# An mLSTM and feed-forward kernel on one core: the opening's 414 steps in another order, with more of the low parts and of the state's decay on GpSimd

## The chip, the core and the metric

The kernel runs on one core of a Trainium2 chip. It has five engines that each run their own instructions in order and wait for each other by semaphores: TensorE (PE, with its weight loads as PEld), VectorE (DVE), ScalarE (ACT), GpSimd (POOL) and SyncE (SP), which here issues nearly all transfers. The metric is the time of one execution in microseconds, the median of several runs; lower is better.

## The reference

First an mLSTM over 4 batches, 8 heads, 768 steps and head size 40, with a stabilised exponential gate; then a feed-forward layer over its 3072 tokens of 320 values.

```python
for t in range(S):
    m_new = np.maximum(f_gate[:, :, t] + m, i_gate[:, :, t])
    f_stab = np.exp(f_gate[:, :, t] + m - m_new)
    i_stab = np.exp(i_gate[:, :, t] - m_new)
    m = m_new
    C = f_stab[:, :, None, None] * C + i_stab[:, :, None, None] * np.einsum('bhd,bhe->bhde', vt, kt)
    n = f_stab[:, :, None] * n + i_stab[:, :, None] * kt
    h_tilde = np.einsum('bhde,bhe->bhd', C, qt)
    denom = np.maximum(np.abs(np.einsum('bhd,bhd->bh', n, qt)[:, :, None]), 1.0)
    y[:, :, t] = 1.0 / (1.0 + np.exp(-o_gate[:, :, t])) * h_tilde / denom
...
x = y.transpose(0, 2, 1, 3).reshape(B * S, H * D)
h = x @ w_in                                            # 3072 x 2048
g = np.maximum(h, 0.0) + alpha * np.minimum(h, 0.0)
out = (g @ w_out).astype(np.float32)                    # 3072 x 320
```

`w_in`, `w_out` and `alpha` take part in double precision in the reference; the weights arrive in DRAM as 8-byte numbers.

## The kernel before

**Tiling.** The recurrence is done by chunks of 128 steps: 6 chunks a batch, 24 in all. Within a chunk the scores (keys times queries, by head) are multiplied by a matrix of decays E and applied to the values; what came earlier enters through the state C. Two chunks make a group of 256 tokens; there are 12 groups, and each goes through the feed-forward layer in 8 pairs of 256 hidden values: an up projection (16 matmuls into a tile `ph`), the activation into `g`, and a down projection (12 matmuls into `po`).

**Precision by parts.** Operands of the feed-forward layer are split into a high part and the rest, the low part (`XH`, `XL`; `WH`, `WL`, and `W2` for the last 64 rows of `w_in`; `OH`, `OL`; `gh`, `gl`), and three products of parts are summed. A low part is one subtraction (`low`, line 891, for weights; line 785 for the products' `gl`). Weights come as two 32-bit words: ScalarE scales the high word (`scale`, line 855), then either scales the low word too (`three`, line 865), or VectorE shifts the high one (`shift`, line 871), and VectorE joins both (`join`, lines 877 and 879).

**Order.** Nothing is left to a scheduler. `ORDER` is a string of names; each name stands for a step that issues some instructions, and every engine runs its instructions in the order in which the steps issue them. After `ORDER`, which covers the first batch (chunks 0 to 5) and the first group or two of the feed-forward layer, a repeating `PATTERN` supplies the rest of the order for chunks 6 to 23 and the other groups; a step that `ORDER` has named isn't repeated. The names that matter here, with n the chunk and p the pair of hidden blocks:

- `dq`n, `dv`n, `dL`, `do` load queries and keys, values, decays and output gates. `i`, `r` and `o` with their numbers are blocks of `w_in`, of its last 64 rows, and of `w_out`: `d` loads a block, `s` scales, `x` or `y` is the choice above, `j` joins, `h` and `H` write a high part, `l` and `L` a low part on VectorE, `p` and `P` a low part on GpSimd.
- `qT`n, `kT`n transpose queries and keys on TensorE, `qc`n, `kc`n copy them out on ScalarE. `sp` spreads the decays over the partitions on TensorE (chunks 0 to 3), `ex` takes their exponential, `sc` makes scores, `wg` multiplies them by E, `v`n applies them to the values, `fm`n and `ft`n take the state's part, `ta`n adds both.
- `wd`n weighs the keys, `um`n and `uc`n update the state with them; `uc`n first multiplies the old state by its decay, on the engine that the set `CP` names.
- `gr`, `gg`, `gx`, `gp` gate chunk n: the reciprocal, the gate, the product (`XNP` names the chunks whose product is GpSimd's), and a copy on GpSimd. `x`n transposes the chunk's x on TensorE; `xa`n writes `XH`, `xd`n writes `XL`.
- `U` or `V` with group and pair is an up projection; `R S G K` or `r s g N` follow: the negative part on ScalarE, the activation on VectorE, the high part on ScalarE, and the low part, on VectorE for `K` and on GpSimd for `N`. `D` is the down projection.

**PSUM.** Most small matmul results of the opening take their tile from `psa`, from two tags of two buffers each; a buffer is free again once its last reader is done. Untagged requests alternate between the tags.

Of the kernel before, what the change touches and what calls it, by code (L numbers as in the profile page):

```python
# [17 lines left out]
def kernel(ctx: ExitStack, tc: tile.TileContext, q, k, v, i_gate, f_gate, o_gate, w_in, w_out, alpha, out):  # L18
# [397 lines left out]
    def gated_steps(n, hv):  # L416
# [21 lines left out]
        if b == 0:  # L438
            nc.vector.scalar_tensor_tensor(out=sg, in0=sg, scalar=1.0, in1=rb, op0=ALU.add, op1=ALU.mult)
        else:  # L440
            nc.gpsimd.tensor_tensor(sg, sg, rb, ALU.mult)
# [214 lines left out]
    def first_stacks():  # L656
# [28 lines left out]
    ORDER = """warm18 kfz alT lf0z warm2 warm2 i00d i00s sca0 lf0a lf0b dq0 L0 sp01 qT0 dq1 alC li0 bj0 wt0 bTt kT0 i00x qc0 kc0 ewj
        i01d sca1 bTc ex01 sp00 sc00 qT1 wTt eeL wTc qc1 wd0 li1 lf1a lf1b kT1 sc01 i00j ex00 kc1 eTt Cz eTc sp11 ex11
        dv0 wg01 i01s wd1 L1 um0 uc0 i01x lpa um1 sp10 wg00 gma gmd ex10 i01j i00h fm1 ft1 sc11 do0 sc10 wg10 bj1 wtl
        blt ewl blc i00p o0d o0s r0d o0x gmm gmc r0s r0x v0 wg11 lpb lpc lpd uc1 dq2 qT2 o2d gr0 wlt og1 warm2 wlc r0j
        i11d lpe o0j i01h i01p gg0 qc2 dq3 gx0 gp0 kT2 v1 eel elt elc sp21 kc2 sc21 dL r0H ta1 gr1 gg1 sp20 ex21 qT3
        wg21 i10d dv1 r0h gx1 gp1 r0p r0L ex20 wd2 sc20 wg20 qc3 x0 x1 xa0 xd0 dq4 fm2 wd3 xa1 xd1 i10s F0 ft2 o2s o2y  # L690
        sp31 o0h ex31 kT3 o2j o2h i10y i10j um2 U00 o0l V01 kc3 R00 i11s uc2 i11y i11j o2l do1 i10h i10l sp30 r01 qT4
        qc4 ex30 S00 v2 sc31 i20d i20s ta2 gr2 i20x wg31 o1d og2 gg2 gx2 kT4 i20j kc4 sc30 wg30 G00 K00 i21d fm3 ft3
        s01 i20h o1s i20p i11h i11p o1x r2d o1j i21s i21x sc41 v3 um3 i21j uc3 ta3 dL4 U02 V03 r2s r2y o3d gr3 sc40
        ex41 fm4 R02 dq5 o1h o1l o4d g01 r2j N01 qT5 i21h i21p o3s S02 o3x G02 K02 dL5 wg41 i31d ft4 D00 wd4 dq6 o3j
        qc5 dv2 r2h r2p r03 ex40 o4s r2H D01 o4x gg3 s03 o3h o4j gx3 o5d gp3 wg40 i30d V04 r04 s04 dv3 o4h V05 gp2 x2
        x3 xa2 xd2 o6d do2 wd6 kT5 g04 r2P g03 o3l xa3 r05 o4l s05 v4 xd3 kc5 i31s ta4 N03 N04 i31y i31j i30s o5s o5x
        F1 V10 gr4 r10 um4 uc4 dL6 i30x um6 U11 ex50 R11 o5j s10 uc6 S11 ex51 g10 i31h dL7 i31p sc50 N10 i30j dq7 wg50
        U12 fm5 ft5 o5h sc51 wg51 v5 o7d R12 S12 ta5 D10 G11 K11 o6s o6x gr5 og3 gg5 G12 gx5 gg4 D11 K12 D12 i30h i30l
        gx4 U13 gp5 D02 tp0 do3 U06 o7s gp4 o5l o6j vp0 R13 tp1 g05 S13 G13 N05 K13 o7x o6h D13 vp1 o7j U07 tp2 tp3
        R06 S06 R07 x4 x5 xa5 xd5 D03 D04 D05 S07 o7h o7l G06 K06 o6l D06 xa4 xd4 G07 K07 D07 Z0"""  # L700
# [36 lines left out]
    class FeedForward:  # L737

        def __init__(self, g):
            self.g, self.x, self.done, self.named = g, x_tiles.pop(g), [], 0  # L740
# [4 lines left out]
        def up(self):  # L745
            for step in self.up_steps(self.g < 2):
                pass

        def up_steps(self, split=True):
            g, fp = self.g, self.named  # L750
            self.named += 1
# [34 lines left out]
            self.done.append((gh, gl))  # L786
# [580 lines left out]
```

## Time and profile before

| | |
|---|---|
| median of 3 runs | 465.4 us (465.05 to 465.82) |
| the profiled execution | 465.35 us, its span 463.6 us |
| granted TensorE clock | 0.998 |
| busy: PE, DVE, ACT, POOL | 452.8, 329.8, 315.0, 308.4 us |
| transfers | 68.67 MB, mean 148 GB/s |

Busy time is that of the span from the first to the last instruction on the core; the execution's own time has 1.75 us more around it. A busy TensorE is not one at its peak, since the ends of matmuls are modelled and overlap. The opening, up to the step that ends `ORDER`, covers about the first 105 us.

### The profile page before, as it was taken

The numbers are of one execution on the slowest core, as the hardware profiler recorded it, in microseconds if no ns is written. First come the engines' busy times: TensorE is split into PE (matmuls) and PEld (weight loads), VectorE is DVE, ScalarE is ACT, GpSimd is POOL, SyncE is SP. The second block draws the span as 40 slices with busy tenths as digits, with TensorE's granted clock in tenths as the row PEclk, the third lists the DMA queues.
The fourth block names the chain that finished last, engine by engine and source line by source line (L and its number), as shares of the span: only waits on it lengthen the run. The fifth ranks groups of instructions, "written<-read, shape, count | busy, mean of one in ns | idle before, by whom it ended". The sixth has DMA issues, their size and how long they took to land.

```text
span 463.6 us, 11813 instructions
## 1 busy us (share of the span) xinstructions
PE 452.8 (98%) x4366; PEld 442.0 (95%) x4366; DVE 329.8 (71%) x692; ACT 315.0 (68%) x707; POOL 308.4 (67%) x377
## 2 busy tenths in 40 slices
PE   8989989999999999999999999999999999999996
PEld 6879978999999999999999999999999999999996
DVE  4989998747776787886875887886776786764321
ACT  4899898676857858758856958757857858423331
POOL 8551674854698697588888598588888686324231
PEclk9999999999999999999999999999999999999999
DMA  9999994869775775888997686688796463020000
GB/s 184 177 221 252 277 252 118 175 122 190 151 182 147 138 184 160 137 174 173 158 187 176 122 197 168 133 166 180 153 206 156 107 154 90 1 84 15 28 2 28
DMA packets 186306, 68.67 MB, mean 148 GB/s; under 512 B 150234, under 2 KB 178506, under 8 KB 186250
## 3 DMA queue, kind: packets, MB, share of 16 engines
q1 hardware_dynamic: 186170, 67.83, 67.2%
q8 instruction: 34, 0.56, 0.5%
q14 instruction: 22, 0.18, 0.2%
q10 hardware_dynamic: 80, 0.11, 0.1%
HBM read 40.44 MB, written 7.57 MB: 104 GB/s over the span
## 4 chain that ended last, share of the span: by engine, by line
PE 83%; DVE 5%; DMA 5%; SPq 3%; ACT 3%; issue 1%; ACTq 0%; DVEq 0%
PE po L796 36%; PE ph L759 5%; PE ph L765 5%; PE ph L762 5%; PE ph L760 5%; PE ph L761 5%; PE ph L764 4%; PE ph L763 4%; PE ph L766 4%; PE pH L377 4%; PE pS L515 4%; DMA wi<-in_moe_w_in_dram 2%; DMA wr<-in_moe_w_in_dram 2%; PE pI L403 1%; PE pu L203 1%; DMA qn<-in_q_dram 1%
## 5 line engine op out<-in xcount | busy, mean ns | idle before, releaser
L785 POOL TENSOR_TENSOR gl<-g,gh 128x512 fp32r<-128x512 f32 x77 | 100.5, 1306 | 42.9 <-ACT gh L783 39.6
L796 PE MATMUL po<-OH,gh 128*128 128x320 f32 x368 | 110.7, 312 | 0.0
L796 PE MATMUL po<-OL,gh 128*128 128x320 f32 x368 | 109.3, 309 | 0.0
L769 ACT ACTIVATE g<-ph 128x512 f32<-128x512 f32 x96 | 57.1, 596 | 58.2 <-PE ph L766 56.0
L774 DVE SCALAR_TENSOR_TENSOR g<-g,oma,ph 128x256 f32<-128x256 f32 x156 | 66.8, 469 | 32.7 <-ACT g L769 32.3
L796 PEld LDWEIGHTS po<-OL,gh 128*128 128x128 f32 x368 | 69.2, 188 | 0.1
L796 PEld LDWEIGHTS po<-OH,gh 128*128 128x128 f32 x368 | 69.1, 188 | 0.0
L796 PE MATMUL po<-OH,gl 128*128 128x320 f32 x368 | 69.0, 309 | 0.0
L759 PE MATMUL ph<-XH,WH 128*128 128x256 f32 x192 | 57.2, 298 | 1.1 <-ACT wo L865 0.7
L796 PEld LDWEIGHTS po<-OH,gl 128*128 128x128 f32 x368 | 57.9, 188 | 0.0
L764 PE MATMUL ph<-XL,WH 128*128 128x256 f32 x192 | 54.3, 283 | 0.9 <-DVE XL L623 0.9
L765 PE MATMUL ph<-XL,WH 128*128 128x256 f32 x192 | 54.3, 283 | 0.0
L762 PE MATMUL ph<-XH,WL 128*128 128x256 f32 x192 | 54.3, 283 | 0.0
L760 PE MATMUL ph<-XH,WH 128*128 128x256 f32 x192 | 54.1, 282 | 0.0
L761 PE MATMUL ph<-XH,WL 128*128 128x256 f32 x192 | 54.1, 282 | 0.0
L364 ACT CAST E<-pS 128x512 bf16<-128x512 f32 x72 | 41.6, 582 | 18.0 <-DVE pS L361 14.0
L763 PE MATMUL ph<-XH,W 128*128 128x256 f32 x192 | 53.4, 278 | 0.2 <-POOL W L891 0.2
L766 PE MATMUL ph<-XL,W 128*128 128x256 f32 x192 | 53.4, 278 | 0.0
L783 ACT CAST gh<-g 128x512 fp32r<-128x512 f32 x77 | 46.5, 618 | 9.1 <-DVE g L774 6.6
L486 ACT ACTIVATE E<-Lb,bT 128x128 f32<-128x128 f32 x160 | 50.0, 392 | 0.0
L361 DVE TENSOR_TENSOR pS<-pS,E 128x512 f32<-128x512 f32 x36 | 24.8, 690 | 29.6 <-PE pS L515 26.2
L759 PEld LDWEIGHTS ph<-XH,WH 128*128 128x128 f32 x192 | 36.1, 188 | 2.0 <-ACT wo L865 0.9
(197 smaller groups left out, 1123.2 us busy)
## 6 DMA issues: line engine op xcount, KB each, us to landing
Lb<-L_d SPq DMA_DIRECT2D x20, 512.0 KB
wo<-in_moe_w_out_dram SPq DMA_DIRECT2D x8, 640.0 KB
wi<-in_moe_w_in_dram SPq DMA_DIRECT2D x8, 512.0 KB
qn<-in_q_dram SPq DMA_DIRECT2D x24, 160.0 KB
kn<-in_k_dram SPq DMA_DIRECT2D x24, 160.0 KB
va<-in_v_dram SPq DMA_DIRECT2D x24, 160.0 KB
og<-in_o_gate_dram SPq DMA_DIRECT2D x24, 160.0 KB
out_dram<-ob SPq DMA_DIRECT2D x11, 320.0 KB
```

The source lines that it names most:

```text
L759: nc.tensor.matmul(dst, WH[half][:, 0, hs], XH[:, 0], start=True, stop=False)
L760: nc.tensor.matmul(dst, WH[half][:, 1, hs], XH[:, 1], start=False, stop=False)
L761: nc.tensor.matmul(dst, WL[half][:, 0, hs], XH[:, 0], start=False, stop=False)
L762: nc.tensor.matmul(dst, WL[half][:, 1, hs], XH[:, 1], start=False, stop=False)
L763: nc.tensor.matmul(dst, W2[:, fs], X2, start=False, stop=False)
L764: nc.tensor.matmul(dst, WH[half][:, 0, hs], XL[:, 0], start=False, stop=False)
L765: nc.tensor.matmul(dst, WH[half][:, 1, hs], XL[:, 1], start=False, stop=False)
L766: nc.tensor.matmul(dst, W2[:, fs], X2L, start=False, stop=True)
L769: nc.scalar.activation(gt, ph, AF.Relu, scale=-1.0)
L774: nc.vector.scalar_tensor_tensor(out=y[:, e], in0=gt[:, e], scalar=oma[:, f : f + 1], in1=ph[:, e], op0=ALU.mult, op1=ALU.add)
L785: (nc.vector if split else nc.gpsimd).tensor_tensor(gl, y, gh.bitcast(F32), ALU.subtract)
L796: nc.tensor.matmul(po[j], x[:, e, j * P : (j + 1) * P], W[f // NB][:, f % NB], **ends)
```

## The change

The string `ORDER` is written anew: 420 names in place of 414, of which 31 old ones go and 37 come, and nearly all the others stand elsewhere. What the names that differ do:

- low parts of weights move from VectorE to GpSimd (`o0`, `o1`, `o2`, `o4`, `o5` and `i10`: `l` becomes `p`), and two the other way (`i01`, and the second piece of `r2`);
- four pairs (pair 2 of group 0; 1, 2 and 3 of group 1) take the form `V r s g N` instead of `U R S G K`, so that their activation goes to SBUF and their low part is GpSimd's;
- the decay of the state is GpSimd's in chunks 1, 2 and 4; the weighting of keys of chunk 1 becomes VectorE's; the product with the gate becomes GpSimd's for chunk 1 and VectorE's for chunk 3;
- the gate of chunk 2 is opened by an addition on GpSimd (`ga2`) and multiplied there; the other `ga` names issue nothing;
- three blocks (`i20`, `r0`, `o7`) are shifted on VectorE instead of having their low word scaled on ScalarE.

A list gives the PSUM tag of each of the opening's first 50 untagged requests, and an up projection is told its pair, so that pairs can be ended out of turn. What follows `ORDER` is the same, step for step.

```diff
     turns = ["b", "a"]
+    first_turns = list("abababbaabababbaabaabaabaabbaabbbaabbaabbabaabbabba")
...
     def psa(name, tag=None):
+        if tag is None and first_turns:
+            tag = first_turns.pop(0)
...
+    def open_gate_early(n):
+        if n in OGP:
+            sg = o_tiles[0][:, n]
+            nc.gpsimd.tensor_scalar(sg, sg, 1.0, None, ALU.add)
...
         if b == 0:
-            nc.vector.scalar_tensor_tensor(out=sg, in0=sg, scalar=1.0, in1=rb, op0=ALU.add, op1=ALU.mult)
+            if n in OGP:
+                nc.gpsimd.tensor_tensor(sg, sg, rb, ALU.mult)
+            else:
+                nc.vector.scalar_tensor_tensor(out=sg, in0=sg, scalar=1.0, in1=rb, op0=ALU.add, op1=ALU.mult)
...
-    XNP = range(2, NBF)
-    KDP = range(1, 24)
-    CP = range(6, 24)
+    XNP = (1, 2, 4, 5)
+    KDP = range(2, 24)
+    CP = (1, 2, 4, *range(6, 24))
+    OGP = range(2, 3)
...
-    ORDER = """warm18 kfz alT lf0z warm2 warm2 i00d i00s sca0 lf0a lf0b dq0 L0 sp01 qT0 dq1 alC li0 bj0 wt0 bTt kT0 i00x qc0 kc0 ewj
+    ORDER = """warm18 sca0 alT lf0z lf0a i00d li0 lf0b dq0 L0 warm2 alC bj0 kfz qT0 sp01 kT0 i00s dq1 bTt i01d i00x qc0 kc0
...
-            g, fp = self.g, self.named
-            self.named += 1
+            g = self.g
...
-            self.done.append((gh, gl))
+            self.done[fp] = gh, gl
```

**Place 1: the transfer queue of SyncE, chunk 2's queries (first `qn` row, into buffer 75) to the group after.** `wo` is a block of `w_out`, `wi_0` and `wi_1` blocks of `w_in`, `va` the values of two chunks, `qn_76` and `kn_78` chunk 3's queries and keys. Before:

```order
L106 DMA qn_75<-in_q_dram 128x8x40
L106 DMA kn_77<-in_k_dram 128x8x40
L928 DMA wo_398<-in_moe_w_out_dram 128x2x640
L845 DMA wi_1_415<-in_moe_w_in_dram 128x1024
L106 DMA qn_76<-in_q_dram 128x8x40
L106 DMA kn_78<-in_k_dram 128x8x40
```

Now:

```order
L109 DMA qn_75<-in_q_dram 128x8x40
L109 DMA kn_77<-in_k_dram 128x8x40
L122 DMA va_80<-in_v_dram 128x8x40 x2
L936 DMA wo_436<-in_moe_w_out_dram 128x2x640
L853 DMA wi_0_464<-in_moe_w_in_dram 128x1024
L853 DMA wi_0_478<-in_moe_w_in_dram 128x1024
L109 DMA qn_76<-in_q_dram 128x8x40
L109 DMA kn_78<-in_k_dram 128x8x40
```

The values of chunks 2 and 3 and one more block of `w_in` now stand ahead of chunk 3's queries.

**Place 2: TensorE around chunk 3's queries and the first up projection.** `pqk_0` is a transpose of queries, `pqk_1` of keys, `pS` scores, `p_0` the transposes of x, `pI` the state's part, `pu` an update of the state, `ph_0` the up projection. Before:

```order
L266 MATMUL pqk_0_481<-ident,qn_76 104x128 x4
L1097 MATMUL pS_0_503<-qf_422,kf_133 128x128 x4
L605 MATMUL p_0_511<-ident,xn_400 128x128 x2
...
L397 MATMUL pI_527<-C_86,qf_422 128x126 x3
...
L266 MATMUL pqk_1_557<-ident,kn_78 104x128 x4
L203 MATMUL pu_568<-va_80,kd_501 40x42 x8
L759 MATMUL ph_0_577<-XH_519,WH_102 128x256
```

Now:

```order
L1105 MATMUL pS_0_483<-qf_413,kf_133 128x128 x4
L274 MATMUL pqk_0_491<-ident,qn_76 104x128 x4
L616 MATMUL p_0_506<-ident,xn_424 128x128 x2
...
L405 MATMUL pI_527<-C_86,qf_413 128x126 x3
...
L767 MATMUL ph_0_548<-XH_521,WH_102 128x256
...
L211 MATMUL pu_571<-va_80,kd_444 40x42 x8
L274 MATMUL pqk_1_581<-ident,kn_78 104x128 x4
```

The scores of chunk 2 go ahead of chunk 3's queries, which now come right before the transposes of x; chunk 3's keys and the update of the state go behind the first up projection.

**Place 3: GpSimd from the low part of the last rows of `w_in` (`W_73`) on.** `kd` are weighted keys, `xn` a gated chunk, `OL` and `WL` low parts of weights, `C` the state, `E` decays, `gl` a product's low part. Before:

```order
L891 TENSOR_TENSOR W_73<-t_wr_371,W_73 64x512
L172 TENSOR_TENSOR kd_501<-kn_77,wT 128x320
L172 TENSOR_TENSOR kd_532<-kn_78,wT 128x320
L443 TENSOR_TENSOR xn_670<-T_540,og_341 128x320
L891 TENSOR_TENSOR WL_711<-t_wi_0_667,WH_710 128x512
L891 TENSOR_TENSOR WL_103<-t_wi_1_616,WH_102 128x512
L489 AFFINE_SELECT E_1_805<-E_1_805 128x512
L785 TENSOR_TENSOR gl_1_825<-g_1_635,gh_1_824 128x512
```

Now:

```order
L899 TENSOR_TENSOR W_73<-t_wr_390,W_73 64x512
L899 TENSOR_TENSOR OL_105<-t_wo_358,OH_104 128x640
L218 TENSOR_TENSOR C_87<-C_86,gamB 104x336
L899 TENSOR_TENSOR OL_618<-t_wo_525,OH_617 128x640
L899 TENSOR_TENSOR WL_103<-t_wi_0_513,WH_102 128x512
L180 TENSOR_TENSOR kd_660<-kn_78,wT 128x320
L151 TENSOR_SCALAR og_310<-og_310 128x320
L448 TENSOR_TENSOR og_310<-og_310,r_673 128x320
L454 TENSOR_TENSOR xn_672<-T_540,og_310 128x320
L899 TENSOR_TENSOR WL_725<-t_wi_0_620,WH_724 128x512
L899 TENSOR_TENSOR WL_103<-t_wi_1_644,WH_102 128x512
L500 AFFINE_SELECT E_1_741<-E_1_741 128x512
```

Two low parts of `w_out`, one of `w_in`, a decay of the state and a gate stand between the same steps as before; chunk 2's keys are weighted ahead of this piece, no longer in it.

More of the change, by code (lines that the diff above doesn't have):

```diff
@@ L679 @@
     BEHIND = 4
-    XNP = range(2, NBF)
-    KDP = range(1, 24)
-    CP = range(6, 24)
+    XNP = (1, 2, 4, 5)
+    KDP = range(2, 24)
+    CP = (1, 2, 4, *range(6, 24))
+    OGP = range(2, 3)
     OBA = range(0)
     WIDE = 3 * VA
-    ORDER = """warm18 kfz alT lf0z warm2 warm2 i00d i00s sca0 lf0a lf0b dq0 L0 sp01 qT0 dq1 alC li0 bj0 wt0 bTt kT0 i00x qc0 kc0 ewj
[L686 to L700, printed above, removed]
@@ L739, in __init__ @@
         def __init__(self, g):
-            self.g, self.x, self.done, self.named = g, x_tiles.pop(g), [], 0
+            self.g, self.x, self.done = g, x_tiles.pop(g), {}
             if g == 1:
@@ L743, in __init__, with up_steps @@
                 self.po = [ps_a.tile([P, 512], F32, tag="b", name=f"po{g}_{j}")[:, :DM] for j in range(GC)]
[L745 to L749, printed above, removed]
-            g, fp = self.g, self.named
-            self.named += 1
+        def up_steps(self, fp, split):
+            g = self.g
             XH, XL, X2, X2L = self.x
@@ L1245, in chunk_steps @@
                 add(f"fm{n} ft{n}", lazily(lambda: state_part(n)))
+            steps[f"ga{n}"] = lambda: open_gate_early(n)
             add(f"gr{n} gg{n} gx{n} gp{n}", lazily(lambda: gated_steps(n, got["T" if n else "h", n])))
@@ L1306, in named_ffn @@
                 for tokens, split in (("URSGK", True), ("VrsgN", False)):
-                    add(" ".join(f"{x}{g}{fp}" for x in tokens), lazily(lambda split=split: ffs[g].up_steps(split)))
+                    add(" ".join(f"{x}{g}{fp}" for x in tokens), lazily(lambda fp=fp, split=split: ffs[g].up_steps(fp, split)))
                 steps[f"D{g}{fp}"] = lambda fp=fp: ffs[g].down(fp)
```

16 lines of the change are left out of this document (added).

## The prediction

> **What bounds the kernel now.** I read the page's first line, then busy time by stretch, then TensorE's waits, then the rows where they stand.
>
> ```profile
> PE 452.8 (98%) x4366; PEld 442.0 (95%) x4366; DVE 329.8 (71%) x692; ACT 315.0 (68%) x707; POOL 308.4 (67%) x377
> ```
>
> TensorE is busy for 98% of the span. By stretch (columns: stretch and length, then busy time and instructions of PE, PEld, DVE, ACT, POOL; granted clock; DMA share; GB/s):
>
> ```profile
> 0.00:50.00 50.00, 45.63 (x415) 40.31 (x416) 39.87 (x85) 41.04 (x94) 26.29 (x46) 1.00 1.00 215
> 50.00:100.00 50.00, 47.12 (x390) 45.86 (x390) 39.00 (x76) 40.31 (x87) 33.04 (x37) 1.00 0.82 189
> 100.00:150.00 50.00, 50.00 (x493) 49.24 (x492) 35.66 (x77) 34.04 (x79) 35.93 (x44) 1.00 0.72 160
> ```
>
> TensorE idles 4.37 us in the first 50 us, 2.88 us in the next 50, and none in the third. After the opening the order is the same before and after and TensorE is full, so the end moves by as much as its idle time in the opening does. That is at most 4.37 + 2.88 = 7.25 us as shown, and 1.4 us of it is the start, where nothing can run. These are the waits, over the whole program (line waited for, releaser, total us, times, longest):
>
> ```profile
> PE warm L160 <- POOL ident masks.py:199: 1.4, 1, 1.4
> PE ph L764 <- DVE XL L623: 0.9, 1, 0.9
> PE pb L100 <- DVE xn L443: 0.8, 1, 0.8
> PE pH L337 <- DVE E L1101: 0.8, 2, 0.6
> PE ph L759 <- ACT wo L865: 0.7, 1, 0.7
> PE ps_gw L1022 <- ACT E L1080: 0.5, 1, 0.5
> PE ps_ge L1022 <- ACT g_WH L1227: 0.4, 1, 0.4
> PE ph L759 <- DVE g L774: 0.4, 1, 0.4
> ```
>
> No wait is over 1.4 us and each has a releaser of its own: there is no one stall to remove. Five stretches show who is short when:
>
> ```profile
> 35.00:40.00 5.00, 5.00 (x46) 4.84 (x45) 4.71 (x11) 4.96 (x12) 0.00 (x0) 1.00 1.01 214
> 45.00:50.00 5.00, 4.82 (x53) 4.46 (x52) 4.77 (x9) 4.84 (x10) 3.56 (x3) 1.00 1.13 271
> 60.00:65.00 5.00, 4.30 (x38) 4.13 (x37) 3.94 (x10) 3.91 (x9) 3.85 (x5) 1.00 0.99 292
> 65.00:70.00 5.00, 4.07 (x60) 3.70 (x58) 4.87 (x11) 4.95 (x11) 3.18 (x2) 1.00 1.13 242
> 75.00:80.00 5.00, 4.29 (x36) 3.95 (x35) 3.45 (x6) 4.70 (x11) 3.66 (x5) 1.00 0.34 99
> ```
>
> From 35 us VectorE and ScalarE are full while GpSimd has nothing at all; TensorE then runs dry between 60 and 80 us (0.70 + 0.93 + 0.71 us in the last three rows). The queue of transfers is full too until 70 us (share 1.01, 1.13, 0.99, 1.13).
>
> **The work that changes engine.** Prices, from groups of the first 170 us (count, busy us, mean ns, idle before):
>
> ```profile
> L891 DVE TENSOR_TENSOR OL<-t_wo,OH 128x640 fp32r<-128x640 f32 x8 | 7.0, 891 | 0.0
> L785 DVE TENSOR_TENSOR gl<-ph,gh 128x512 fp32r<-128x512 f32 x6 | 4.1, 682 | 0.7 <-ACT gh L783 0.7
> L221 DVE TENSOR_TENSOR C<-C,gamB 40x168 f32<-40x168 f32 x8 | 2.5, 318 | 0.1
> L785 POOL TENSOR_TENSOR gl<-g,gh 128x512 fp32r<-128x512 f32 x16 | 21.7, 1358 | 8.6 <-ACT gh L783 8.6
> L891 POOL TENSOR_TENSOR WL<-t_wi,WH 128x512 fp32r<-128x512 f32 x6 | 8.2, 1371 | 1.6 <-ACT WH L887 1.5
> L230 POOL TENSOR_TENSOR C<-C,gamB 40x336 f32<-40x336 f32 x4 | 3.0, 751 | 0.0
> L865 ACT ACTIVATE wi<-wi 128x512 uint32<-128x512 uint32 x5 | 3.4, 676 | 0.0
> ```
>
> VectorE loses five low parts of w_out (5 x 0.89 = 4.5), four of products (4 x 0.68 = 2.7), one of w_in (0.68) and three decays of two instructions (6 x 0.32 = 1.9): 9.8 us. Some small steps go both ways (a gate and a product with the gate to GpSimd; a weighting of keys, another such product, two low parts and three shifts to VectorE) and by the like prices give back about 3. Net: some 7 us less for VectorE. GpSimd takes the same at its own price: 5 x 1.71 (1.37 scaled from 512 to 640 columns), 4 x 1.36, 1.37 and 3 x 0.75, with the small steps some 15 us more. ScalarE loses three scalings of a low word, about 0.7 each, 2 us in all, of which one lies between 35 and 66 us.
>
> **Term 1, up to the first up projection (group 0, pair 0).** The new order makes some of this work earlier and some later.
>
> Earlier: the wait of 0.8 us on xn is for a bank of PSUM that the values of chunk 0 still hold; the new list of banks puts that matmul (chunk 2's spread) on a bank that a copied query has left. The 0.4 us on g_WH go too, since that spread then comes ahead. That is 1.2 us of the waits between 22 and 29 us.
>
> Later: the queries of chunk 0 now stand ahead of the first spread.
>
> ```profile
> 5.70 0.38 PE L100 MATMUL pb<-later,ident 128*128 128x512 bf16 x1
> 6.25 1.16 PE L1052 MATMUL pb<-g_L,ident 128*128 128x128 f32 x8 [0.17 <-DVE g_L L1153]
> 7.24 0.60 PE L266 MATMUL pqk<-ident,qn 128*104 128x128 f32 x4
> ```
>
> Before, the spread fills 5.7 to 7.2 us; when the queries arrived the trace does not show, only that they were there at 7.24. If they are there at 5.7 nothing is lost; if only at 7.1, the spread (0.22 + 1.0) starts when it used to end and up to 1.2 us are lost. I take 1.0, since the transfers behind them come one by one (below).
>
> The larger piece is chunk 3's queries. They were transfer rows 16 and 17 after the loads of chunk 2, behind one block of w_out and one of w_in; now two blocks of w_in and the values of chunks 2 and 3 stand ahead too (512 and 320 KB more). What the queue carried from 0 to 22.9 us, from there to 30 us, and to 33 us (packets, MB, share):
>
> ```profile
> q1 hardware_dynamic: 11176, 4.02, 98.6%
> q1 hardware_dynamic: 2778, 2.07, 108.2%
> q1 hardware_dynamic: 5682, 2.55, 106.9%
> ```
>
> It is full all along. Chunk 2's queries end a wait of TensorE at 22.89 us (below), which dates the queue. From them to chunk 3's queries the new order has 160 (keys) + 320 + 640 + 2 x 512 + 160 = 2304 KB = 2.36 MB. At 2.07/7.1 = 0.292 MB per us that takes 8.1 us, at 2.55/10.1 = 0.252 it takes 9.4: arrival at 31.0 to 32.3, and I take 31.6. Before it was 1472 KB = 1.51 MB, 28.1 to 28.9.
>
> ```profile
> 22.89 0.61 PE L266 MATMUL pqk<-ident,qn 128*104 128x128 f32 x4 [0.37 <-DMA qn<-in_q_dram]
> 29.89 0.60 PE L266 MATMUL pqk<-ident,qn 128*104 128x128 f32 x4
> 31.22 1.21 PE L605 MATMUL p<-ident,xn 128*128 128x128 f32 x6
> 34.94 0.38 PE L759 MATMUL ph<-XH,WH 128*128 128x256 f32 x1
> ```
>
> Before, TensorE took them at 29.89 without a wait, did the last scores of chunk 2 (0.9) and began the transposes of x at 31.22. In the new order these scores come first and the queries after, so TensorE is ready for them at about 30.8 and waits to 31.7; the transposes begin at 32.2, 1.0 us later than before. Whatever else is saved earlier is lost in this wait. What follows the transposes on ScalarE:
>
> ```profile
> 32.01 0.37 ACT L618 CAST XH<-p 128x256 fp32r<-128x256 f32 x1 [0.19 <-PE p L605]
> 33.03 0.37 ACT L618 CAST XH<-p 128x256 fp32r<-128x256 f32 x1 [0.30 <-DVE XL L623]
> ```
>
> Before, the second half of x is cast at 33.0. Now the copy of the late queries stands ahead of the first half, and a scaling of w_out (0.8) between the halves, so the second comes at about 34.3 and the projection at 35.1, with two pieces that ran ahead of it (keys of chunk 3, update of chunk 2; 34.0 to 34.9 before) now behind it. Done with all three, TensorE is **1.1 us later** than before. Ends: all waits of the first 35 us but the start gone and the queries early, 4.37 - 0.18 (the row from 45 us) = 4.2, less 1.4, 2.8 us better; or arrival at 32.3 and the loss at the head passed on in full, 2.5 worse.
>
> **Term 2, from there to 85 us.** TensorE's idle time here is 7.25 - 4.2 = 3.1 us. Each wait costs some 0.1 more than it shows, since the first matmul after one is followed late: about 3.9 us in all. VectorE comes to the second group's x (the 0.9 us on XL) with some 5 of its 7 us less in front of it; ScalarE with 0.7 less, and 1.09 us of idle between 60 and 65 to use. So the wait on XL and those on a slot of ph (0.7 and 0.4) go for the most part, and half of the 0.8 us on E: I take **2.9 us gained** of 3.9. Ends: none of it, and 3.9.
>
> **Term 3, GpSimd.** Its 15 us more fit where it had nothing to do:
>
> ```profile
> 44.91 1.13 POOL L443 TENSOR_TENSOR xn<-T,og 128x320 f32<-128x320 f32 x1 [10.03 <-DVE og L439]
> ```
>
> Ten idle us stand ahead of this one product. I put its cost at nothing. Between the first projection and the copy that completes chunk 3's x, 35 to 62 us before, it is given nine low parts (3 x 1.71 + 5 x 1.37 + 1.36 = 13.3 us) and ten small steps of 0.6 to 1.1 (8): 21 us, so 6 us of cover are left. If the cover is gone, that copy is late next (rival (c)). After 85 us the order is the same, and 0 is taken there.
>
> Sum: 1.1 - 2.9 = -1.8 us. The profiled execution took 465.35 us (span 463.6 and 1.75 around it), 0.05 under the median of 465.4; 465.35 - 1.8 gives **463.5 us**.
>
> **Rivals.** *(a) The queries don't hold it up*: the queue drains faster, or they are used late enough. For it: the blocked issue behind chunk 2's weighting of keys goes, as that step moves forward; against it: that block lies behind the queries in the queue. Then term 1 is -1 to 0 and term 2 keeps its 2.9 to 3.9: about 461.3.
>
> *(b) VectorE is not relieved*, since GpSimd's work is in its way. Two gates of the same shape, and GpSimd's row beside the first:
>
> ```profile
> 25.92 1.55 DVE L439 SCALAR_TENSOR_TENSOR og<-og,r 128x320 f32<-128x320 f32 x1
> 29.09 0.49 DVE L439 SCALAR_TENSOR_TENSOR og<-og,r 128x320 f32<-128x320 f32 x1
> 25.86 1.26 POOL L891 TENSOR_TENSOR WL<-t_wi,WH 128x512 fp32r<-128x512 f32 x1 [0.55 <-ACT WH L887]
> ```
>
> The first ends 0.35 us after GpSimd's product does, and is 1.06 us longer than the second, which ran alone. From 35 to 66 us VectorE has about a dozen such joins and gates with both inputs in SBUF; if half of them are newly met at 0.7 to 1.06, 4 to 6 us come back, all that was taken off there. Term 2 falls to about -0.9: 465.35 + 1.1 - 0.9 = 465.5, no change. Against it: the sums from PSUM, which are most of VectorE's work there, are the same 0.68 us either way, and ScalarE is the fuller engine. [...]
>
> *(c) GpSimd becomes the bound*, the case that ends slower. It works in order, and the copy that completes x of chunk 3 is now behind four more long steps. If GpSimd waits more than 6 us for its inputs between 35 and 62 us, that copy is late by the rest, and so are ScalarE's cast, VectorE's difference and the second group's first projection. At 9 us of such waits it is 3 late, and the gain of term 2 is gone: 465.35 + 1.1 + 1.5 (the part that other projections can't fill) is about 468. For it: 10.0 us of waiting in one piece before. Against it: that wait was for lack of work, with VectorE behind.
>
> That the kernel doesn't do what its title says is no rival: the steps that change engine stand in the instruction order.
>
> **How the numbers follow.** Forecast 0.45, (a) 0.20, (b) 0.17, (c) 0.18. Its own range, 462 to 465, is widened to (a)'s and (c)'s nearer halves: 460.6 to 466.8. A difference under 0.2% (0.93 us) can't be told from none here. Faster by more: 0.40 of the forecast, all of (a), 0.02 of (b): 0.62. Within: 0.05 + 0.13 + 0.02 = 0.20. Slower: 0.02 of (b) and 0.16 of (c): 0.18.
>
> **What would show it.** Term 1: a wait of TensorE on a transfer of q of about 1 us near 31 us, and the first ph near 35. Term 2: idle time of TensorE between 37 and 85 us near 1 us instead of 3.1, and no wait on XL at the second group. Term 3: GpSimd's waits short between 35 and 62 us, TensorE never released by a GpSimd copy. (b) would show as gates and joins over 1 us on VectorE from 35 to 66 us; (c) as a wait on the second transposes of x. I am wrong if TensorE's idle time after 85 us grows, or if the first 35 us gain.

## The result, and the profile after

| | before | after | after, a second set |
|---|---|---|---|
| median | 465.1 us | 468.1 us | 466.6 us |
| lowest to highest, runs | 464.0 to 465.8, 20 | 465.4 to 470.3, 20 | 465.4 to 470.1, 10 |
| ratio to before, 95% interval | | 1.0065 [1.0051, 1.0079] | 1.0037 [1.0016, 1.0059] |

The second set is the first experiment below; its kernel before, on the same chip, took 464.8 us. The change makes the kernel slower, by 0.4 to 0.65%, where 0.4% faster was forecast. It also spreads it: before lies within 1.8 us, after within 4.9. Two executions among the experiments took 733 us at a mean clock of 0.56 and are left out of every median, ratio and span below.

The profiled execution after took 465.4 us (span 463.3) and is the fastest of the 20. It shows what the change does to the order, but not the whole loss: 465.4 is no slower than before. The page's first line:

```profile
PE 452.8 (98%) x4366; PEld 442.4 (95%) x4366; DVE 322.3 (70%) x681; ACT 314.2 (68%) x704; POOL 324.3 (70%) x389
```

The shift of work is the one forecast: VectorE 7.5 us less (329.8 before), GpSimd 15.9 more (308.4). Busy time up to 35 us, about where the forecast's first term ends, and in the 50 us behind it (stretch and length, then PE, PEld, DVE, ACT, POOL, granted clock, DMA share, GB/s), after:

```profile
0.00:35.00 35.00, 31.82 (x273) 27.62 (x273) 25.62 (x59) 27.19 (x66) 21.22 (x42) 1.00 1.05 212
35.00:85.00 50.00, 45.78 (x422) 44.03 (x421) 41.87 (x78) 42.51 (x85) 37.69 (x34) 1.00 0.80 201
```

and before:

```profile
0.00:35.00 35.00, 30.81 (x278) 26.09 (x278) 25.52 (x57) 26.27 (x63) 22.64 (x43) 1.00 0.97 193
35.00:85.00 50.00, 46.94 (x415) 45.09 (x414) 45.06 (x90) 43.15 (x90) 25.49 (x25) 1.00 0.89 226
```

What TensorE idles is the length less its busy time. In the first 35 us that is 3.18 us after and 4.19 before, so the head gained 1.0. In the next 50 us VectorE has 3.2 us less to do, yet TensorE idles 4.22 us, and 3.06 before; the forecast was about 1. The idle time of this execution has not gone, it has new places. The waits of TensorE (start, length, instruction, idle time before it and its releaser):

```profile
6.82 0.62 PE L274 MATMUL pqk<-ident,qn 128*104 128x128 f32 x4 [0.94 <-DMA qn<-in_q_dram]
30.28 0.62 PE L274 MATMUL pqk<-ident,qn 128*104 128x128 f32 x4 [0.30 <-DMA qn<-in_q_dram]
33.03 0.39 PE L767 MATMUL ph<-XH,WH 128*128 128x256 f32 x1
43.04 1.16 PE L1105 MATMUL pS<-qf,kf 104*128 104x128 f32 x8 [0.88 <-DVE T L1242]
59.55 0.38 PE L770 MATMUL ph<-XH,WL 128*128 128x256 f32 x1 [0.85 <-POOL WL L899]
61.22 0.39 PE L771 MATMUL ph<-XH,W 128*128 128x256 f32 x1 [1.29 <-POOL W L899]
70.57 0.81 PE L211 MATMUL pu<-va,kd 128*40 128x42 f32 x32 [1.00 <-DMA va<-in_v_dram]
```

The waits of before on XL (0.9), on xn (0.8) and on a slot of `ph` are gone. In their place TensorE waits twice for low parts of weights on GpSimd at 59 to 61 us, once for the sum T at 43, and once for values at 70. The two at 59 to 61 us and the one at 70, 0.85 + 1.29 + 1.00 = 3.1 us, lead to two steps on GpSimd, by way of SyncE's queue and of GpSimd's own order. The rows of SyncE after:

```profile
36.06 0.38 SPq L109 DMA_DIRECT2D qn<-in_q_dram  x1
41.46 0.37 SPq L109 DMA_DIRECT2D kn<-in_k_dram  x1
41.92 0.78 SPq L129 DMA_DIRECT2D Lb<-L_d  x1
...
49.32 0.42 SPq L109 DMA_DIRECT2D qn<-in_q_dram  x1
58.29 0.37 SPq L109 DMA_DIRECT2D kn<-in_k_dram  x1
...
59.33 1.09 SPq L122 DMA_DIRECT2D va<-in_v_dram  x2
```

SyncE issues the queries and then stands in front of the keys: for 5.0 us after 36.4, and for 8.6 us after 49.7. What it waits for are two steps on GpSimd, the weighting of the keys of chunks 3 and 4, whose ends free the buffers into which the next keys but one are loaded:

```profile
40.53 0.90 POOL L180 TENSOR_TENSOR kd<-kn,wT 128x320 f32<-128x320 f32 x1
...
57.54 0.72 POOL L180 TENSOR_TENSOR kd<-kn,wT 128x320 f32<-128x320 f32 x1
58.22 1.27 POOL L899 TENSOR_TENSOR WL<-t_wi,WH 128x512 fp32r<-128x512 f32 x1
59.57 1.60 POOL L899 TENSOR_TENSOR W<-t_wr,W 64x512 fp32r<-64x512 f32 x1
```

They end at 41.43 and 58.26, and the loads of keys are issued 0.03 us later. While SyncE stands, everything behind it stands too: the decays of chunk 4, then blocks of weights and the values that TensorE misses at 70.57. On ScalarE the decays are 2.38 us late:

```profile
48.61 1.28 ACT L497 ACTIVATE E<-Lb,bT 128x128 f32<-128x128 f32 x4 [2.38 <-DMA Lb<-L_d]
```

Before, ScalarE scaled the weights of these two low parts (47.84 and 48.99 us) ahead of the decays' exponential at 49.56; the new order has them behind it (50.97 and 52.11). So what holds up the decays holds up these weights too. GpSimd then takes the second weighting of keys right ahead of the two low parts, and TensorE waits for them. The kernel before had a block of this kind too:

```profile
52.15 0.38 SPq L106 DMA_DIRECT2D qn<-in_q_dram  x1
56.71 0.37 SPq L106 DMA_DIRECT2D kn<-in_k_dram  x1
```

But the decays had been issued ahead of it at 39.20, and its weighting of chunk 3's keys was done by 34.9.

### The profile page after: what moved, and what is told of

Same layout as the page of the kernel before. It is cut to its first block, busy times and chain, and to the rows that moved or that the text cites. A ratio compares the mean times of both kernels' runs of the same rounds, so it can differ in the third digit from the quotient of the medians.

```text
span 463.3 us, 11810 instructions
## 1 busy us (share of the span) xinstructions
PE 452.8 (98%) x4366; PEld 442.4 (95%) x4366; DVE 322.3 (70%) x681; ACT 314.2 (68%) x704; POOL 324.3 (70%) x389
## 4 chain that ended last, share of the span: by engine, by line
PE 88%; DMA 5%; ACT 2%; SPq 1%; POOL 1%; issue 1%; DVE 0%; POOLq 0%; ACTq 0%
PE po L804 36%; PE ph L767 5%; PE ph L770 5%; PE ph L773 5%; PE ph L768 5%; PE ph L769 5%; PE ph L772 5%; PE ph L771 4%; PE ph L774 4%; PE pH L385 4%; PE pS L526 4%; DMA qn<-in_q_dram 3%; PE pu L211 2%; DMA Lb<-L_d 1%; PE pS L1105 1%; PE pI L411 1%
## 5 line engine op out<-in xcount | busy, mean ns | idle before, releaser
L793 POOL TENSOR_TENSOR gl<-g,gh 128x512 fp32r<-128x512 f32 x78 | 101.1, 1298 | 38.8 <-ACT gh L791 35.7
L782 DVE SCALAR_TENSOR_TENSOR g<-g,oma,ph 128x256 f32<-128x256 f32 x164 | 70.3, 470 | 35.3 <-ACT g L777 34.9
L771 PEld LDWEIGHTS ph<-XH,W 128*128 128x128 f32 x192 | 36.8, 191 | 1.5 <-POOL W L899 1.5
```

Of the source, the lines that this page charges most:

```text
L771: nc.tensor.matmul(dst, W2[:, fs], X2, start=False, stop=False)
L782: nc.vector.scalar_tensor_tensor(out=y[:, e], in0=gt[:, e], scalar=oma[:, f : f + 1], in1=ph[:, e], op0=ALU.mult, op1=ALU.add)
L793: (nc.vector if split else nc.gpsimd).tensor_tensor(gl, y, gh.bitcast(F32), ALU.subtract)
```

## The experiments

Each has a ratio to the kernel before, taken on the same chip. Beside the time stands what every run reports: the span and the mean granted clock. The kernel before, in its 100 runs beside the experiments, has a span of 462.1 to 464.6 us, the median 463.1, and a mean clock of 0.998 to 1.000 (in one run 0.95, with a span of 463.6 like the others).

### The same kernel again

> The changed kernel as it stands. In its 20 timed executions the span goes with the granted clock: 463.3 to 464.3 us at a clock of 1.000, 465 to 468 at 0.989 to 0.996. Theory A (the clock): TensorE's clock is granted at half for a stretch in most executions, so the ones with a clock under 0.997 are 2 us or more longer than those at 1.000, the kernel before shows a clock of 0.998 to 1.000 throughout, and a profile that falls on a slow one shows the stretch. Theory B (waits alone): spans differ as much among executions at one and the same clock, and the clock is a by-product.

466.56 us, 1.0037 [1.0016, 1.0059]. Slower again, though less so. With the first set, the runs fall into groups by their mean clock:

| mean granted clock | runs of 30 | median span |
|---|---|---|
| 0.999 or 1.000 | 14 | 464.2 us |
| 0.995 or 0.996 | 6 | 465.8 us |
| 0.989 to 0.993 | 10 | 466.8 us |

Where a profile below has the clock at half, it is for 3.4 us at a time or twice that: 61.84 to 65.25 us, 3.41, in the kernel before with late places. One such piece lowers the mean over 464 us by 0.0037 (3.41 / 2 / 464). So by their means, an estimate, 16 of 30 runs of this kernel have one to three pieces at half clock; the two profiled runs have none. By these medians the loss against before has three parts: 1.1 us in the span at a mean of 0.999 or 1.000 (464.2 against 463.1), 1.6 for the first piece at half clock and less for the next, and some 0.4 outside the span (2.09 against 1.71 us).

The first part is a mixture. The 14 spans of the first group run from 463.3 to 466.0 us at a clock of 0.999 or 1.000, so theory B holds for a part of the spread. One reason is visible, in the first matmuls of the start, first in the profile after, then in this one:

```profile
7.49 1.05 PE L1060 MATMUL pb<-g_L,ident 128*128 128x128 f32 x8
```

```profile
8.03 1.91 PE L1060 MATMUL pb<-g_L,ident 128*128 128x128 f32 x8
```

The same eight matmuls take nearly twice as long. In the second profile the transposes of keys behind them, at 9.73 us, take 1.06 us, in the first 0.60 (at 8.38); the next eight of the same shape, at 11.42 us, take 1.05. The view by stretch grants this piece, 5.00 to 10.79 us, a clock of 1.00, so the mean of 1.000 shows nothing of it. At 38 us the second is 1.8 us behind (chunk 3's queries are transposed at 37.86, not 36.03), and its span is 464.8 against 463.3. In ten other profiles of this study the first eight such matmuls take 1.05 to 1.38 us; how often a slow start comes in the runs without a profile isn't known.

### Does the wait at the start cost the clock?

```diff
-dq0 L0 warm2 alC bj0 kfz qT0 sp01 kT0
+dq0 L0 warm10 alC bj0 kfz qT0 sp01 kT0
```

> Eight more of the idle-time matmuls are put ahead of the first transpose of queries, where TensorE waits about 1 us for a transfer at 5.6 to 6.8 us; they compute nothing that is used. Theory A, with its cause in that early wait: the clock comes back to 0.998 to 1.000 in nearly all executions, and the median falls from 468.1 to about 465.5. If the clock is lost elsewhere (the waits at 43, 59 to 61 or 70 us), clock and median stay at 0.993 to 0.996 and 468. Theory B: no change, 468.

467.05 us, 1.0042 [1.0018, 1.0066]: nothing gained. The wait of 0.94 us for the first queries, filled with matmuls whose result isn't used, does not bring the clock back: four of nine runs still have a mean clock of 0.989 to 0.996. In its profile the half clock stands from 61.8 to 68.6 us, twice 3.4, and begins during the second of the two waits for low parts (1.14 us up to 60.82, 1.30 up to 62.50). This rules the wait at the start out as the cause of the half clock. Whether the start costs time by slow first matmuls, it doesn't tell.

### The head of the order back as it was

```diff
-first_turns = list("abababbaab...
+first_turns = list("aabbabbaab...
-alC bj0 kfz qT0 sp01 kT0
+alC bj0 kfz sp01 qT0 kT0
```

> The one step of the first spread goes back ahead of the queries' transpose, with the same PSUM banks. My prediction put 1.0 us of loss on this swap. By theory A with the early wait as its cause: clock back to 0.998 to 1.000, 465 us. By a loss that is only the time of the wait: 0.5 to 1 us less than the changed kernel at the same clock. If the head is slack: no change.

466.38 us, 1.0034 [1.0017, 1.0051]: no better than the change itself by more than the intervals, and seven of ten runs have a mean clock of 0.989 or 0.996. Here the profiled run is one of them, and the view by stretch shows the half clock. First this kernel, then the second set of the changed one, whose profiled run has none:

```profile
63.00:66.40 3.40, 3.40 (x18) 3.39 (x18) 1.87 (x4) 2.72 (x5) 3.40 (x5) 0.50 1.13 274
```

```profile
63.00:66.40 3.40, 2.89 (x24) 2.89 (x25) 2.63 (x4) 3.40 (x9) 2.33 (x5) 1.00 1.05 273
```

At half clock TensorE does 18 matmuls in 3.40 us; at full clock, with 0.5 us idle, 24. The two waits ahead were 0.80 + 1.43 us in the first and 1.31 + 1.31 in the second: the smaller sum has half clock behind it in one execution, from 62.96 us on, and the larger none in another. What makes the difference, the two don't show.

### Low parts back to VectorE

```diff
-D01 i21p r2H r2h wg41 r2p o5d
+D01 i21l r2H r2h wg41 r2l o5d
```

> Two low parts of weights (the fourth block's of w_in, i21, and the first piece of its last rows, r2) go back from GpSimd to VectorE at the same places in the order. In the profile of the changed kernel TensorE waits 0.85 and 1.29 us for just these two at 58 to 61 us. If GpSimd's lateness is what eats the gain, these 2.1 us of waiting go and the span falls by 1 to 2 us at an equal clock. If VectorE or ScalarE is as late, the wait is only renamed and the time stays within 0.5 us.

467.35 us, 1.0045 [1.0026, 1.0064]. Of the 2.14 us of waits at 59 to 61 us, 0.56 + 0.94 stay, now on VectorE, and a wait of 1.23 us on a high part of x comes in at 69.14. Only three of ten runs have a mean clock under 0.999 (0.995 and 0.996), but the time is no better. So GpSimd's price for these two parts is not the main cause: they are late on either engine.

### The keys weighted earlier

```diff
-sc31 i10p i20y i11y i20j og2 qc4 wd3 ga2 G00
+sc31 wd4 i10p i20y i11y i20j og2 qc4 ga2 G00
-qc3 x1 r0p xa0
+qc3 x1 r0p wd3 xa0
-s02 r03 wd4 o3j dq6
+s02 r03 o3j dq6
```

> The weightings of chunk 3's and chunk 4's keys (wd3, wd4) go forward on GpSimd, to behind r0p and to ahead of i10p; all else is the changed kernel. In its profile SyncE sits 5.0 us (36.4 to 41.5) on the load of chunk 5's keys and 8.5 us (49.7 to 58.3) on chunk 6's, whose buffers these weightings free; all loads behind them come late (decays of chunk 4, the last rows of w_in, values). Theory C: this blocked queue is what turned the gain into a loss, through ScalarE's 2.4 us of waiting for decays, the late low parts at 58 to 62 us, the 1.0 us on values at 70 us, and the halved clock after them. Then the two blocks are gone, TensorE's waits from 55 to 75 us shrink from 3.1 to under 1.5 us, the clock is 0.998 to 1.000 in nearly all executions, and the median falls to 463 to 465. If the queue is not the cause, the waits stay and the median is 466 to 468.

464.85 us, 0.9992 [0.9976, 1.0007]: two steps of 0.7 us each, moved on GpSimd alone, take back the whole loss. By the ratios that is 0.45% or 2.1 us against the second set (1.0037), and 3.4 us against the first. In this kernel the keys follow the queries:

```profile
36.25 0.38 SPq L109 DMA_DIRECT2D qn<-in_q_dram  x1
36.74 1.13 SPq L109 DMA_DIRECT2D kn<-in_k_dram  x1
37.95 3.46 SPq L129 DMA_DIRECT2D Lb<-L_d  x1
```

and after 40 us TensorE has three waits over 0.5 us, these two and one of 0.54 us on the state's C at 73.08:

```profile
43.23 1.16 PE L1104 MATMUL pS<-qf,kf 104*128 104x128 f32 x8 [1.02 <-DVE T L1241]
59.92 0.39 PE L770 MATMUL ph<-XH,W 128*128 128x256 f32 x1 [0.91 <-POOL W L898]
```

From 55 to 75 us the waits are 1.76 us in sum, against 3.1 and somewhat over the 1.5 expected. By which of the two ways the steps do it, these rows tell in part:

```profile
48.18 1.28 ACT L497 ACTIVATE E<-Lb,bT 128x128 f32<-128x128 f32 x4 [1.77 <-DMA Lb<-L_d]
56.75 1.60 POOL L898 TENSOR_TENSOR WL<-t_wi,WH 128x512 fp32r<-128x512 f32 x1 [0.24 <-ACT WH L894]
```

The load of the decays lasts 3.46 us in the queue here, so ScalarE has them only 0.43 us earlier than in the changed kernel. Yet the first of the two low parts starts 1.47 us earlier (56.75 against 58.22). So some 0.4 us came by way of the queue, and the rest by GpSimd's own order: the weighting of 0.7 us no longer stands right ahead, and the copy before it took 0.23 us, not 0.91. The wait for values at 70 us has gone with the queue; they are issued at 57.64, not 59.33. No run parts the two ways within the changed kernel.

Six of the 12 runs have a mean clock of 0.999 or 1.000, with a span of 461.8 us in the median: 1.3 below before. The other six have 0.996, and took 463.7, so the clock did not come back in nearly all executions as expected. The profile holds no wait that explains these six.

### Both of these together

> As keys_early, and with the first spread ahead of the queries' transpose. If both causes hold (blocked queue, and the wait at 5.6 to 6.8 us that lets the first full clock come late in some executions) this is the fastest and steadiest: 462.5 to 464.5, spread under 2 us. If the early wait is harmless it equals keys_early.

464.33 us, 0.9989 [0.9975, 1.0003], no different from the one before, and not the steadiest: four of 11 runs have a mean clock of 0.992 or 0.996. The head of the order is worth nothing that these runs can tell.

### The engines alone, and the order alone

One kernel has the order of before with the engines of the change (the low parts, the state's decay, the gates), and one nearly the reverse, the new order and banks with the engines of before, but for four pairs that keep their new form.

> The order of before, with only the steps' engines and forms of the changed kernel (low parts, decays of the state, gates, four pairs, three shifts), and PSUM banks in turn as before. If moving work to GpSimd is good in itself, and the new order spoils it: 463.5 to 464.5. If the moves cost (VectorE held up by GpSimd, GpSimd late): over 465.5.

> The new order and PSUM banks with the engines of before (decays, gates, low parts and the low words' scaling), except for the four pairs, which the new order needs in their new form. If the order is what loses: 467 or more, with the same block of SyncE behind chunk 3's keys. If the engines lose: 465 or less.

The engines alone: 477.68 us, 1.0254 [1.0226, 1.0281], the worst kernel of all, with a mean clock of 0.989 in three of four runs and 0.996 in the other. GpSimd's work, put where VectorE's stood, makes three waits of about 2 us in its profile, the third of 2.1 us for a low part of g at 103 us. Behind the first two the matmuls of 128x256 start 0.21 us apart and not 0.12, from 63.3 to 66.7 and from 73.5 to 77.0 us; the mean clock, 0.989, is that of three such pieces at half clock. The first two:

```profile
61.99 0.39 PE L770 MATMUL ph<-XH,W 128*128 128x256 f32 x1 [2.28 <-POOL W L898]
72.47 0.39 PE L771 MATMUL ph<-XL,WH 128*128 128x256 f32 x1 [1.90 <-DVE XL L634]
```

The order alone: 464.42 us, 0.9990 [0.9978, 1.0001], span 462.7 us in the median and a mean clock of 0.998 to 1.000 in all 10 runs. With less ahead of it on GpSimd, the same late place of the keys' weighting blocks SyncE for 1.0 and 4.7 us (36.7 to 37.7, 50.7 to 55.4) instead of 5.0 and 8.6, and TensorE idles 1.60 us between 35 and 85 us instead of 4.22. So the order by itself brings most of the relief there that was forecast for the whole change, and yet its time is not clear of before. The loss is not in the order alone: it needs the engine to be free, and the engine's new work needs the order.

### The late places in the kernel before

```diff
-dq4 fm2 wd3 xa1 xd1          -ft4 D00 wd4 dq6      -ta3 dL4 U02 ... R02 dq5 o1h
+dq4 fm2 xa1 xd1              +ft4 D00 dq6          +ta3 dq5 dL4 U02 ... R02 o1h
-og2 gg2 gx2 kT4              -o4s r2H D01
+og2 gg2 gx2 wd3 kT4          +o4s r2H wd4 D01
```

> The kernel before, with its own engines and order, and three steps put where the change put them: the weighting of chunk 3's keys behind chunk 2's gate, that of chunk 4's keys ten steps later, and chunk 5's loads ahead of chunk 4's decay. SyncE's queue should then show the stretches without an issue that the changed kernel has (its 36.4 to 41.5 us and 49.7 to 58.3 us; in the kernel before 30.8 to 34.2 and 52.5 to 56.7). If the blocked queue alone harms: 466 to 467.5 us, ratio 1.002 to 1.005, and new waits of TensorE for weights or their low parts at 55 to 70 us. If it harms only where GpSimd has more work ahead of the weighting (the two together): 464.8 to 465.4 us, ratio 0.9995 to 1.0005.

468.5 us, 1.0079 [1.0064, 1.0094]: three steps out of 414 in the kernel before (the two weightings later, and chunk 5's loads ahead of chunk 4's decays), each engine with the work it had, cost more than the whole change does. Of the two stretches without an issue that were expected, one comes, and it is enough. SyncE stands from 39.2 to 46.06, until GpSimd has weighted the keys; GpSimd came to that only then, since it works in order and a product ahead had waited 10.69 us:

```profile
44.23 1.13 POOL L443 TENSOR_TENSOR xn<-T,og 128x320 f32<-128x320 f32 x1 [10.69 <-PE pI L397]
45.31 0.72 POOL L172 TENSOR_TENSOR kd<-kn,wT 128x320 f32<-128x320 f32 x1
```

```profile
38.66 0.54 SPq L106 DMA_DIRECT2D qn<-in_q_dram  x1
46.06 0.37 SPq L106 DMA_DIRECT2D kn<-in_k_dram  x1
```

```profile
52.59 1.28 ACT L486 ACTIVATE E<-Lb,bT 128x128 f32<-128x128 f32 x4 [3.33 <-DMA Lb<-L_d]
```

```profile
59.86 0.38 PE L760 MATMUL ph<-XH,WH 128*128 128x256 f32 x1 [1.86 <-DVE gl L786]
61.88 0.58 PE L764 MATMUL ph<-XH,W 128*128 128x256 f32 x1 [1.28 <-POOL W L892]
```

The chain is that of the changed kernel: late keys, decays issued at 46.49 instead of 39.20 and 3.33 us late on ScalarE, waits of 3.1 us at 58 to 62, and the clock at half from 61.84 to 65.25; five of six runs have a mean clock of 0.991 or 0.996. GpSimd has no new low part here, so this way is shown by itself: the blocked queue alone harms, and the cost lies above the expected 466 to 467.5.

### The new order with early keys and the engines of before

> The new order with the engines of the kernel before (464.42 us in its own run, SyncE without an issue 36.7 to 37.7 and 50.7 to 55.4 us), and the weighting of the keys of chunks 3 and 4 early on GpSimd as well. If what is left of the order's gain is lost in that queue: 462.5 to 463.8 us, ratio 0.994 to 0.9975, with no stretch over 2 us without an issue ahead of a load of keys. If the queue does no more harm once GpSimd is relieved: 464.0 to 464.8 us, ratio 0.998 to 0.9995.

464.14 us, 0.9995 [0.9979, 1.0010]. The second reading holds: with GpSimd relieved, the block that is left costs nothing that can be measured. The profiled run also still had a stretch without an issue ahead of a load of keys (37.3 to 39.3 us), which the expectation had excluded for the first reading.

### Is VectorE held up by GpSimd?

From the kernel with early keys, one low part (i10) goes back to VectorE. The other letter (i20x for i20y) takes a shift off VectorE and has ScalarE scale the low word instead; the join that the expectation names is not given back.

```diff
-sc31 wd4 i10p i20y i11y
+sc31 wd4 i10l i20x i11y
```

> The changed kernel with the keys weighted early (464.85 us in its own run), and two steps of the first experts' weights given back to VectorE: the low part of expert 1's first half, and a join of expert 2's. That leaves GpSimd idle while VectorE does the two shifts at about 39 us that took 2.11 us each in the changed kernel. If GpSimd's running there is what lengthens them, they take about 0.4 to 0.5 us each, the wait of TensorE on the transposed product at 43 us (1.02 us) falls under 0.4 us, and the time is 463.9 to 464.6 us. If VectorE's own load is what makes the product late, its longer list costs as much as is gained: the wait stays at 0.8 to 1.3 us and the time is 464.7 to 465.4 us.

464.12 us, 0.9985 [0.9973, 0.9996]. It is the one kernel of this study whose interval lies below 1, by 0.04 to 0.27%. In the changed kernel two shifts of VectorE took 2.11 us, 1.06 each, while GpSimd wrote a low part; then the same stretch where VectorE writes that low part itself, and GpSimd has nothing from 43.2 to 44.5 us:

```profile
39.61 2.11 DVE L879 TENSOR_SCALAR t_wi<-t_wi 128x512 uint32<-128x512 uint32 x2
41.64 0.93 DVE L887 SCALAR_TENSOR_TENSOR t_wi<-wi,t_wi 128x512 uint32<-128x512 uint32 x1
42.49 0.49 DVE L1242 TENSOR_TENSOR T<-T,pH 128x336 f32<-128x336 f32 x1
```

```profile
39.29 1.27 POOL L899 TENSOR_TENSOR WL<-t_wi,WH 128x512 fp32r<-128x512 f32 x1
```

```profile
41.74 1.01 DVE L782 SCALAR_TENSOR_TENSOR ph<-g,oma,ph 128x256 f32<-128x256 f32 x2
42.79 0.96 DVE L899 TENSOR_TENSOR WL<-t_wi,WH 128x512 fp32r<-128x512 f32 x1
43.68 0.41 DVE L879 TENSOR_SCALAR t_wi<-t_wi 128x512 uint32<-128x512 uint32 x1
44.01 0.68 DVE L885 SCALAR_TENSOR_TENSOR t_wi<-t_wi,wi 128x512 uint32<-128x512 uint32 x1
44.62 0.49 DVE L1242 TENSOR_TENSOR T<-T,pH 128x336 f32<-128x336 f32 x1
```

A shift takes 0.41 us alone, so GpSimd's running is what lengthens it. From the activation's row (L782) to T it is 2.9 us here, and was 3.9 in the changed kernel (38.56 to 42.49), with a low part more on VectorE and a shift less; TensorE's wait for T is gone. How much of that is the hindrance and how much the shift that went, this run doesn't part. The time moves by less than the intervals (0.9992 to 0.9985), so what this wait was worth isn't resolved.

### What is outside the span

The last kernel gives the two low parts of the fourth experiment back to VectorE as well.

> The kernel with the keys weighted early and two steps of the first experts given back to VectorE (464.12 us, ratio 0.9985 to the kernel before), with two more low parts of the weights, of experts 2 and 0, given back to VectorE. Two questions. First the time outside the span: 2.04 to 2.12 us in that kernel, 1.59 to 1.68 in the one that gave these two low parts back in the changed kernel. If these two steps decide it, it is 1.6 to 1.7 us here, and the time falls to 463.4 to 463.9 us, ratio 0.9970 to 0.9982; if not, it stays at 2.05 to 2.12 us. Second, the queue of SyncE no longer being blocked, whether VectorE can take the two low parts: if it can, the span stays at about 461.9 us in the median; if it is late for the weights' low parts then (as where it gave them, 0.56 and 0.94 us of waits for VectorE at 59 to 61 us), the span is 462.8 to 464 us and the time 464.5 to 465.7 us.

464.48 us, 0.9998 [0.9984, 1.0013]. The first question has an answer. The time outside the span falls to 1.58 to 1.67 us, so in this order these two instructions decide it. The time does not follow to the 463.4 to 463.9 us expected: among the runs with a mean clock of 0.999 or 1.000 the span is 462.75 us in the median, and was 461.9. That VectorE pays for the two low parts isn't shown by it, since the intervals overlap and the profile has no wait for them at 59 to 61 us. Why they decide what is outside the span is open: it isn't GpSimd's number of instructions alone, since the engines-alone kernel has the 389 of the changed one and 1.6 us.

## Why the prediction was wrong

**Term 1, +1.1 us: the sign was wrong in the first profile, the size small.** The start lost what was put down (a wait of 0.94 us at 6.82; 1.0 was taken). The queries of chunk 3 came at 30.28 us and TensorE waited 0.30 us for them, where arrival at 31.0 to 32.3 and a wait of 0.9 were worked out. The first up projection began at 33.03, not 35.1. Some of that is order: an update and a transpose of keys came ahead of it before and stand behind it now. With all three done TensorE goes on at 36.03, and did at 36.93 before: 0.9 earlier, not 1.1 later. "The first 35 us gain" was named as a sign of being wrong, and they do gain, 1.0 us. But this piece changes from execution to execution. In the second profile the first matmuls are slow (1.91 us for the eight at 8.03) and TensorE is 0.9 us later than before at the same point, and in two profiles of kernels with early keys the queries come at 32.1 us after a wait of 2.16 and of 1.89 us, near what the working had.

**Term 2, -2.9 us: the named waits went, others came.** There is no wait on XL at the second group and none on a slot of `ph`, as forecast. But TensorE idles 4.22 us between 35 and 85 us (4.25 in the second profile), against 3.06 before and the 1 forecast. The gain itself was no mistake, as the 1.60 us of the order alone show. The working asked which waits of before are relieved, and not what the moved steps make late.

**Term 3, "I put its cost at nothing": this step failed.** It counted GpSimd's 15 us against idle time in a piece of 10, and 6 us of cover for one consumer, the copy of chunk 3's x. The consumers that mattered were others. The weighting of the keys stands later in the new order, among the new low parts. Its end frees a buffer for which SyncE waits with the whole queue behind it, 5.0 and 8.6 us long; and it stands itself ahead of two low parts that TensorE needs. The prediction knew the first mechanism: in rival (a) it said that the blocked issue behind *chunk 2's* weighting goes, since that step moves forward. It did not follow the same step for chunks 3 and 4, which move back. Late places alone, in the kernel before, cost 3.9 us; taking the two weightings out of the change brings it from 1.0037 to 0.9992, some 2.1 us. Shown is that their late places are the cause. How the loss divides between the queue and GpSimd's own order is open in the changed kernel.

**The rest of the loss is the clock, in 16 of 30 runs.** The forecast put 0.1 us on each wait beyond what it shows; in the kernel before, the matmul after the one that ends a wait starts 0.23 and 0.20 us behind it (at 58.85 and 61.25 us), where others start 0.12 apart. The two waits at 59 to 61 us can cost another 1.6, by 3.4 us at half clock. How much idle time it takes, the profiles don't show. Half clock stood from 62.96 us in the kernel with the old head, with 1.60 us of TensorE's idle time in the 3.41 us ahead of it, and from 61.84 in the kernel before with late places, with 2.68. But the profile after has 2.15 us of idle time between 58.68 and 62.09 us, and its clock stays at 1.00. Nor is it the length of one wait: with early keys and the old head a wait of 2.16 us for chunk 3's queries, up to 32.11 us, had none behind it, and with early keys and i10 back on VectorE one of 1.89 us, up to 32.12, had half clock from 32.3 to 35.7. So the two sums above stay unexplained, and the loss differs from execution to execution. So do the six runs with early keys at 0.996: their kernel's profile, of a run at 1.000, has no wait over 1.02 us after 40 us.

**Rival (a)** was right for the changed kernel's two profiles that the queries would not hold TensorE up (waits of 0.30 us and none), but its 461.3 us needed the gain to stay. That gain exists: with early keys and a mean clock of 0.999 or 1.000 the span is 461.8 us, 1.3 below before, where the forecast was 1.8. Half the runs keep it, and some 0.4 us goes outside the span.

**Rival (b)** was right that VectorE's steps last longer beside GpSimd's, with too large a price. Over the first ten profiles of this study, first 110 us, a shift of w_in's word takes 420 ns in the median alone and 977 where GpSimd runs, a join of w_out 817 and 1116, the gate 491 and 1084; sums from PSUM stay (678 and 681). In the profile before, two such shifts take 0.42 and 0.43 us where GpSimd has nothing (36.14 and 39.42), and one at 68.3 beside GpSimd 0.87. In the changed kernel it is argued to have made one wait, 0.88 us at 43, where 4 to 6 us had been worked out as given back.

**Rival (c)** had the engine and the sign. Its place was wrong: the copy of chunk 3's x held nothing up, and no wait on the second transposes of x is in the profile. That its time, 468, is near the first set is luck, since it was added up from waits that did not come.

Of the signs named ahead, "TensorE never released by a GpSimd copy" holds, but the weights' low parts of GpSimd release it twice. TensorE's idle time after 85 us did not grow: there is no wait of it there.

## What to carry to other kernels

A compute step whose end frees a buffer is an input of the transfer queue: when such a step moves back, or its engine gets more work ahead of it, follow every load queued behind the one that waits for the buffer, and every step behind it on its own engine, not only its readers. When several small waits are to be traded for others, look at how near they lie to each other: 1.60 us of idle time within 3.41 us, in the kernel with the old head, had 3.4 us at half clock behind it, which cost nearly as much again. And work moved to an idle engine needs a new order of that engine: the engines alone were 2.5% slower, and the order alone no different from before.

## What was not expected of the hardware

- Waits of 1 to 2 us can have 3.4 us at half clock behind them. With 1.60 and 2.68 us of TensorE's idle time in the 3.41 us ahead the clock fell (old head; late places in the kernel before), with 2.15 it did not (the profile after). Of 30 runs of the changed kernel 14 have a mean clock of 0.999 or 1.000, 6 of 0.995 or 0.996, 10 of 0.989 to 0.993; of the kernel before, 99 of 100 have 0.998 or more.
- The half clock can last longer: 6.8 us in the profile with more matmuls at the start, from 61.8 to 68.6. And the first matmuls can be slow: in the second profile of the changed kernel eight of 128x128 take 1.91 us at 8.03, in the first 1.05 at 7.49, and the mean granted clock, 1.000 in both, shows nothing of it. In these two profiles this goes with 1.5 us of span.
- The time outside the span is 1.6 to 1.8 us for some kernels (two runs of before had 1.9 and 2.0) and 2.03 to 2.15 for others, but for the kernel with more matmuls at the start, 2.05 to 3.33. Two instructions moved between engines at 58 us shift it. The cause is open.
- Two low parts that TensorE waits for kept 1.5 of 2.14 us of waiting when VectorE, the faster engine, wrote them (the low part i10 took 0.96 us on it, and 1.27 on GpSimd in the changed kernel). That a slow engine ends a wait does not say that its speed is the reason.
